# One order of attention's steps for another, with the first query load on ScalarE's queue

## The chip, the cores and the metric

The kernel runs on one core of one Trainium2 chip. The metric is the device time of one execution in microseconds (us). Five engines run side by side, each through its own list of instructions in order: TensorE (PE in the profile, with its weight loads as PEld), VectorE (DVE), ScalarE (ACT), GpSimd (POOL) and SyncE (SP), which here only issues DMAs. Engines wait for each other through semaphores alone.

## What is computed

Attention within clusters, then a mixture of experts over its output:

```python
q_assign = argmax(einsum('bhsd,hcd->bhsc', q / |q|, c / |c|))     # 16 clusters a head
k_assign = argmax(einsum('bhsd,hcd->bhsc', k / |k|, c / |c|))
scores = where(q_assign == k_assign, q @ k.T / sqrt(D), -1e9)     # B, H, S, D = 4, 8, 768, 64
x = softmax(scores) @ v                                           # as 3072 x 512
logits = x @ w_gate                                               # 8 experts
# tokens go to experts in order of falling logit, 384 to an expert; then, for each expert:
out[mask] = maximum(x[mask] @ w1[e], 0) @ w2[e]
```

## The kernel before

**Two lists of steps.** The program is written as two long strings of step names, one for attention and one for the experts. The first is named at L21. Each word of the string calls one small function, which issues a few instructions on one engine. So the string sets, by hand, in what order every engine meets its work; nothing else sorts it. Only the first string differs between the two kernels.

**Units.** Attention runs in 8 units u = 0 to 7, each of one batch and 4 heads. Per unit there are 24 tiles, each 128 keys or queries by all 768 of the other side.

- `load,u,k|q|v` fetches a unit by DMA (L488); unit 0's q and k come head by head, 192 KB each. `split_sc` (L630, ScalarE) multiplies a load by 64 in place, `split_hi` (L634, ScalarE) rounds it to half precision, and `split_lo` writes what the rounding lost. With the letter P, `split_lo` runs on GpSimd (L641) and wants the scaled load; with D, `split_hi` scales on its own and `split_lo` runs on VectorE (L639), so that no `split_sc` is needed. `dup` copies the rounded half into a second operand (`qb`, `kb`).
- `c0`, `c1`, `c2,0` to `c2,15`, `c3`, `c4` (L518 to L549) normalize the centroids: a chain of small VectorE operations with one square root on ScalarE (`c1`, L521), two transposes on TensorE (`c3`) and a copy into `ct` (`c4`).
- `cent0` and `cent` (L653) multiply queries and keys by the centroids on TensorE. `hh0` to `hh5` (unit 0) and `hot0` to `hot5` turn the products into cluster marks: four operations on VectorE (L675 to L681), one comparison there (L686) and one copy on ScalarE (L689, L691), which puts the marks beside the data in `qb`, `kb`.
- `pt` and `ptc` (L728, L732 or L734) transpose unit 0 on TensorE and copy the result out; later units are transposed by DMA (`trans`, L722).
- `m_mm` (L770) multiplies for one tile of queries the marked operands of all keys, and `m_rd` (L774, VectorE) takes the maximum of each row. There are 192 of each.
- `row0`, `row1` (L788, L792, VectorE) make three extra rows from the maxima of half a unit, `rowt` (L795) transposes them by DMA, and `row2` (L799) puts them by a second DMA into the query operand `qbt`, where `b_mm` reads them.
- `b_mm` (L809, L813) makes the scores of one tile, `b_exp` (L816, ScalarE) their exponentials, and `res` (L824) what their rounding to bf16 lost, on GpSimd (P) or VectorE (D). `av` (L846, L848, L827) multiplies by the values. `out0`, `out1`, `out2`, `hi0`, `hi1` (L856 to L879) divide and store.
- `m_mm`, `b_mm` and `pt` share three PSUM buffers named `sc`.
- `tab,n` is the n-th of a list of small constants, `offs` (L947) among them; `wgs` (L552, L553) splits the gate's weights. `misc` fills constants on GpSimd.
- `wd` (L660) is a product of 384 columns whose result nobody reads, before and between unit 0's steps.

In the steady part, the steps of unit u's `b_mm`, `b_exp`, `res` and `av` alternate with those of unit u+1's marks, `m_mm` and `m_rd`.

Of the kernel before, what the change touches and what calls it, by code (L numbers as in the profile page):

```python
# [26 lines left out]
split_hi,0,k,3,P split_lo,0,q,1,P wd c4 wd dup,0,q,1 cent0,0,k dup,0,k,1 cent0,0,q tab,14 split_lo,0,k,1,P wd dup,0,q,0
wd hh0,0 wd wd dup,0,k,0 hh1,0 wd split_lo,0,k,2,P wd split_hi,0,q,2,P hh2,0 pt,0,ka,1 pt,0,qa,1 hh3,0 split_sc,0,v,-
tab,12 wd split_lo,0,k,3,P ptc,0,ka,1,D pt,0,ka,2 wd ptc,0,qa,1,D wd wd wd hh4,0,q load,1,q,- wd hh4,0,k
split_hi,0,v,-,P tab,4 cent0,1,k wd wd wd cent0,1,q wd hh5,0,q tab,2 wd hh0,1 split_lo,0,v,-,P hh5,0,k wd split_sc,0,q,3  # L30
pt,0,qb,0 hh1,1 wd ptc,0,ka,2,A pt,0,kb,0 hh2,1 wd wd ptc,0,qb,0,A ptc,0,kb,0,D pt,0,ka,3 wd hh3,1 wd split_sc,1,k,-
m_mm,0,0 hh4,1,k hh4,1,q m_mm,0,1 m_rd,0,0 wd split_lo,0,q,2,P vs,0 load,2,k,- split_hi,0,q,3,P ptc,0,ka,3,D dup,0,k,3
split_lo,0,q,3,P m_rd,0,1 dup,0,k,2 pt,0,qa,2 vact,0 wd wd ptc,0,qa,2,D load,1,v,- vh2,0 m_mm,0,2 wd hh5,1,q vl2,0
pt,0,qa,3 split_hi,1,k,-,P m_rd,0,2 cent0,2,k cent0,2,q m_mm,0,3 hh0,2 wd hh5,1,k wd dup,0,q,2 split_lo,1,k,-,P
ptc,0,qa,3,D wd wd pt,0,qb,1 split_sc,1,q,- hh1,2 wd m_rd,0,3 pt,0,kb,1 wd wd wd hh2,2 wd ptc,0,kb,1,A m_mm,0,4 hh3,2 wd
wd hh4,2,k dup,0,q,3 wd ptc,0,qb,1,D wd wd split_hi,1,q,-,P m_rd,0,4 tab,31 m_mm,0,6 trans,1,ka,- zqm wd wd tab,10 wd
hh4,2,q m_mm,0,5 m_rd,0,6 hh5,2,q cent0,3,k hh5,2,k split_lo,1,q,-,P cent0,3,q m_mm,0,7 m_rd,0,5 wd wd wd wd hh0,3 wd wd
hh1,3 wd wd m_rd,0,7 pt,0,qb,2 m_mm,0,8 ptc,0,qb,2,A wd hh2,3 wd m_mm,0,9 trans,1,qa,- row0,0,0 hh3,3 split_sc,1,v,- wd
row1,0,0 hh4,3,k pt,0,qm,0 hh4,3,q m_rd,0,8 wd cent,1,k,0 ptc,0,qm,0,A cent,1,k,1 m_rd,0,9 cent,1,k,2 cent,1,k,3 hh5,3,q
split_hi,1,v,-,P pt,0,kb,2 hot0,1,k wd pt,0,qb,3 ptc,0,kb,2,D b_mm,0,0 hot1,1,k load,2,q,- hh5,3,k ptc,0,qb,3,A  # L40
pt,0,kb,3 load,2,v,- hot2,1,k wd wd ptc,0,kb,3,D b_exp,0,0 m_mm,0,11 hot3,1,k wd wd dup,1,q,- wd res,0,0,P m_rd,0,11
m_mm,0,10 wd wd m_mm,0,13 hot4,1,k m_mm,0,12 dup,1,k,- m_rd,0,10 split_lo,1,v,-,P cent,1,q,0 cent,1,q,1 wd m_rd,0,13 wd
wd split_hi,2,k,-,D m_mm,0,14 cent,1,q,2 m_rd,0,12 b_mm,0,2 cent,1,q,3 m_rd,0,14 b_exp,0,2 b_mm,0,1 hot0,1,q wd
m_mm,0,15 b_exp,0,1 row1,0,1 wd row0,0,1 hot1,1,q pt,0,qm,1 hot5,1,k tab,5 wd res,0,1,P m_rd,0,15 wd ptc,0,qm,1,A wd
trans,1,kb,- b_mm,0,3 hot2,1,q b_mm,0,5 b_exp,0,3 res,0,2,P hot3,1,q m_mm,0,16 b_exp,0,5 hot4,1,q wd wd m_mm,0,19
m_rd,0,16 hot5,1,q res,0,3,P b_mm,0,4 m_rd,0,19 b_mm,0,6 b_exp,0,4 trans,1,qb,- av,0,0 split_lo,2,k,-,D b_exp,0,6
m_mm,0,17 m_mm,0,18 vs,1 res,0,4,P m_rd,0,17 b_mm,0,7 m_rd,0,18 vact,1 m_mm,0,20 b_exp,0,7 row1,0,2 trans,2,ka,-
row0,0,2 m_mm,0,21 m_rd,0,20 av,0,1 split_hi,2,q,-,D res,0,7,P m_rd,0,21 m_mm,0,22 av,0,2 m_rd,0,22 vh2,1 pt,0,qm,2
res,0,5,P m_mm,0,23 ptc,0,qm,2,A av,0,3 m_rd,0,23 m_mm,1,0 b_mm,0,9 res,0,6,P load,3,k,- vl2,1 m_mm,1,1 m_rd,1,0
b_exp,0,9 av,0,4 av,0,5 m_rd,1,1 b_mm,0,8 row1,0,3 out0,0,0 tab,27 row0,0,3 m_mm,1,2 out1,0,0 b_exp,0,8 out2,0,0,D  # L50
b_mm,0,10 m_rd,1,2 hi0,0,0 cent,2,k,0 res,0,8,P b_mm,0,12 b_exp,0,10 hi1,0,0 m_mm,1,3 b_exp,0,12 m_mm,1,4 m_rd,1,3
res,0,9,P cent,2,k,1 split_hi,2,v,-,D cent,2,k,2 b_mm,0,11 m_rd,1,4 av,0,6 split_lo,2,q,-,D b_exp,0,11 m_mm,1,5 m_mm,1,6
dup,2,k,- cent,2,k,3 b_mm,0,14 m_rd,1,5 res,0,11,P av,0,7 trans,2,qa,- b_exp,0,14 av,0,8 hot0,2,k m_rd,1,6 b_mm,0,13
res,0,10,P av,0,9 hot1,2,k b_exp,0,13 pt,0,qm,3 hot2,2,k res,0,12,P m_mm,1,7 ptc,0,qm,3,A b_mm,0,15 hot3,2,k m_rd,1,7
load,3,q,- av,0,10 b_exp,0,15 res,0,13,P av,0,11 hot4,2,k b_mm,0,17 out0,0,1 out1,0,1 out2,0,1,D m_mm,1,8 res,0,14,P
b_exp,0,17 b_mm,0,16 m_rd,1,8 hi0,0,1 m_mm,1,9 b_exp,0,16 hi1,0,1 m_mm,1,10 res,0,15,P m_rd,1,9 hot5,2,k av,0,12 xtr,0,0
split_hi,3,k,-,D b_mm,0,18 m_rd,1,10 res,0,16,P m_mm,1,11 load,3,v,- av,0,13 m_rd,1,11 b_exp,0,18 m_mm,1,12 res,0,17,P
dup,2,q,- av,0,14 m_rd,1,12 b_mm,0,20 b_mm,0,19 res,0,18,D b_exp,0,20 av,0,15 row1,1,0 b_exp,0,19 row0,1,0
split_lo,2,v,-,D m_mm,1,13 rowt,1,0 lg0,0,0 av,0,16 av,0,17 res,0,19,P m_rd,1,13 b_mm,0,22 b_mm,0,21 out0,0,2 row2,1,0
out1,0,2 b_exp,0,22 tab,1 tab,22 m_mm,1,14 lg1,0,0 res,0,20,P trans,2,kb,- out2,0,2,D b_exp,0,21 cent,2,q,0 cent,2,q,1  # L60
m_rd,1,14 cent,2,q,2 hi0,0,2 cent,2,q,3 b_mm,1,0 res,0,22,P hot0,2,q hi1,0,2 m_mm,1,15 b_exp,1,0 b_mm,1,2 hot1,2,q
res,0,21,P m_rd,1,15 b_mm,0,23 av,0,18 hot2,2,q b_exp,0,23 split_lo,3,k,-,D av,0,19 b_exp,1,2 b_mm,1,1 m_mm,1,17
b_exp,1,1 res,0,23,P hot3,2,q m_mm,1,16 trans,3,ka,- av,0,20 m_rd,1,17 split_hi,3,q,-,D av,0,21 m_rd,1,16 res,1,0,P
m_mm,1,19 av,0,22 hot4,2,q av,0,23 m_rd,1,19 hot5,2,q b_mm,1,3 tab,8 res,1,2,P m_mm,1,18 out0,0,3 out1,0,3 b_exp,1,3
b_mm,1,4 trans,2,qb,- m_rd,1,18 res,1,1,P m_mm,1,20 b_exp,1,4 out2,0,3,D vs,2 hi0,0,3 res,1,3,P hi1,0,3 b_mm,1,5
m_rd,1,20 b_mm,1,6 b_exp,1,5 tab,24 xst,0,0 av,1,0 split_lo,3,q,-,D b_exp,1,6 m_mm,1,21 load,4,k,- av,1,1 vact,2
split_hi,3,v,-,D m_mm,1,22 b_mm,1,7 m_rd,1,21 res,1,6,P av,1,2 vh2,2 m_rd,1,22 m_mm,1,23 b_exp,1,7 res,1,4,P av,1,3
m_rd,1,23 m_mm,2,0 b_mm,1,9 row1,1,1 res,1,5,P m_rd,2,0 b_mm,1,8 b_exp,1,9 av,1,4 vl2,2 b_exp,1,8 m_mm,2,1 row0,1,1
res,1,7,P m_mm,2,2 rowt,1,1 m_rd,2,1 av,1,5 b_mm,1,10 out0,1,0 out1,1,0 res,1,8,P out2,1,0,D b_mm,1,11 b_exp,1,10
m_rd,2,2 cent,3,k,0 row2,1,1 hi0,1,0 cent,3,k,1 res,1,9,P b_exp,1,11 m_mm,2,4 hi1,1,0 xtr,0,1 cent,3,k,2 m_rd,2,4  # L70
dup,3,k,- m_mm,2,3 av,1,6 res,1,10,P m_rd,2,3 m_mm,2,6 trans,3,qa,- b_mm,1,12 m_rd,2,6 cent,3,k,3 res,1,11,P b_exp,1,12
m_mm,2,5 av,1,7 hot0,3,k hot1,3,k b_mm,1,14 res,1,12,P m_rd,2,5 av,1,8 b_exp,1,14 b_mm,1,13 hot2,3,k load,4,q,-
split_lo,3,v,-,D av,1,9 b_exp,1,13 xst,0,1 m_mm,2,7 b_mm,1,15 av,1,10 hot3,3,k res,1,13,P b_exp,1,15 m_rd,2,7 av,1,11
b_mm,1,16 out0,1,1 hot4,3,k res,1,15,P m_mm,2,8 out1,1,1 b_exp,1,16 b_mm,1,17 out2,1,1,D m_rd,2,8 lg0,0,1 hi0,1,1
res,1,16,P b_mm,1,18 b_exp,1,17 hi1,1,1 m_mm,2,9 b_exp,1,18 m_mm,2,11 xtr,1,0 av,1,12 tab,3 res,1,14,P m_rd,2,9
split_hi,4,k,-,D m_mm,2,10 av,1,13 lg1,0,1 m_rd,2,11 load,4,v,- res,1,17,P m_mm,2,12 dup,3,q,- av,1,14 m_rd,2,10 av,1,15
# [1395 lines left out]
```

## Time and profile before

| | us |
|---|---|
| median of 3 runs | 689.34 (689.24 to 691.9) |
| the profiled execution | 689.53 |
| its span, first to last instruction | 687.4 |
| mean granted TensorE clock | 0.976 of full speed |

| engine | busy us | share of the span |
|---|---|---|
| PE | 652.1 | 95% |
| DVE | 510.6 | 74% |
| POOL | 480.2 | 70% |
| ACT | 421.1 | 61% |

The time outside the span is 689.53 - 687.4 = 2.1 us. Attention takes the first 384 us or so, the experts the rest. A row of the timeline gives the start, the length, the engine, the line, what is written from what and how many instructions it stands for; the bracket at its end is the idle time of the engine ahead of it and who ended that. The ends of TensorE's products are modelled, so that a share of 95% does not say that it has no room: gaps shorter than a product's modelled tail are not seen.

### The profile page before, as it was taken

To read this page: it belongs to the slowest core of one execution; us is meant where nothing else is said; L and a number is where in the kernel's file an instruction comes from. 1 tells how busy PE (TensorE), PEld (TensorE's weight loads), DVE (VectorE), ACT (ScalarE), POOL (GpSimd) and SP (SyncE) were. 2 spreads that over 40 slices of the span, in tenths; PEclk is the share of its full clock that TensorE was granted. 3 is DMA by queue.
4 is the path that set the end of the run, shared out by engine and by line. 5 is a ranking of instruction groups with operands and counts; after the bars stand their busy time and mean duration, and the time that the engine had idled before them with its cause. 6 is when DMAs were issued, how large, how long until landed. Compare 5 with 4: busy or idle time off the path is not lost. (4 is left out here: it accounts for less than half of the span.)

```text
span 687.4 us, 19732 instructions
## 1 busy us (share of the span) xinstructions
PE 652.1 (95%) x8256; PEld 435.2 (63%) x8256; DVE 510.6 (74%) x1155; ACT 421.1 (61%) x554; POOL 480.2 (70%) x389
## 2 busy tenths in 40 slices
...
GB/s 197 175 176 149 173 198 135 166 156 182 165 164 142 133 178 203 98 104 89 74 27 71 25 144 150 269 70 315 128 292 140 244 204 179 245 331 175 46 1 46
DMA packets 175450, 105.84 MB, mean 154 GB/s; under 512 B 135426, under 2 KB 160002, under 8 KB 175362
## 3 DMA queue, kind: packets, MB, share of 16 engines
...
q14 instruction: 24, 0.20, 0.1%
...
## 5 line engine op out<-in xcount | busy, mean ns | idle before, releaser
L824 POOL TENSOR_TENSOR rt<-pt 128x768 f16<-128x768 f32 x174 | 260.8, 1524 | 77.8 <-ACT pt L816 72.2
L816 ACT ACTIVATE pt<-sc 128x768 f32<-128x768 f32 x192 | 150.6, 811 | 109.2 <-PE sc L813 106.2
L774 DVE TENSOR_REDUCE mxs<-sc 128x1 f32<-128x768 f32 x192 | 178.3, 949 | 17.0 <-PE sc L770 16.3
L1394 PE MATMUL pf<-xgt,w1h 128*128 128x384 f16 (+1 forms) x640 | 128.8, 293 | 0.3 <-DVE xgt L734 0.3
L846 PE MATMUL av<-vh,pt 128*128 128x66 f16 x1152 | 122.8, 194 | 0.1
L827 PE MATMUL av<-vh,rt 128*128 128x66 f16 x1152 | 122.5, 193 | 0.0
L848 PE MATMUL av<-vl,pt 128*128 128x64 f16 x1152 | 122.5, 192 | 0.0
L846 PEld LDWEIGHTS <-pt 128*128 128x128 bf16 x1152 | 106.4, 98 | 9.1 <-issue 0.2
L848 PEld LDWEIGHTS <-pt 128*128 128x128 bf16 x1152 | 105.8, 98 | 9.3 <-issue 0.9
L827 PEld LDWEIGHTS <-rt 128*128 128x128 f16 x1152 | 105.1, 97 | 0.0
L809 PE MATMUL sc<-qbt,kbt 99*128 99x384 f16 x384 | 93.8, 325 | 5.7 <-DMA qbt<-mt 4.1
L770 PE MATMUL sc<-kbt,qbt 80*128 80x384 f16 x384 | 91.0, 327 | 3.1 <-ACT pt L816 1.2
L813 PE MATMUL sc<-qat,kat 128*128 128x384 f16 x384 | 93.9, 325 | 0.0
L1394 PE MATMUL pf<-xgt,w1l 128*128 128x384 f16 (+1 forms) x320 | 89.9, 293 | 0.0
L1356 ACT ACTIVATE wr<-wr 128x1024 f32<-128x1024 f32 x64 | 66.7, 1046 | 25.2 <-DMA wr<-in_moe_w_dram 25.2
L1394 PEld LDWEIGHTS <-w1h 128*128 128x128 f16 x640 | 57.3, 97 | 28.7 <-issue 1.1
L1432 PE MATMUL pf<-w2h,hh 128*128 128x512 f16 x192 | 72.6, 378 | 0.0
L1432 PE MATMUL pf<-w2l,hh 128*128 128x512 f16 x192 | 72.5, 378 | 0.0
L1432 PE MATMUL pf<-w2h,hl 128*128 128x512 f16 x192 | 72.5, 378 | 0.0
L1366 POOL TENSOR_TENSOR w2l<-wr,w2h 128x1024 f16<-128x1024 f32 x32 | 67.6, 2132 | 1.7 <-ACT w2h L1359 1.2
L1366 POOL TENSOR_TENSOR w1l<-wr,w1h 128x1024 f16<-128x1024 f32 x32 | 67.5, 2137 | 0.2
...
## 6 DMA issues: line engine op xcount, KB each, us to landing
...
xg<-xrow,idx POOLq DMA_INDIRECT x24, 6.3
```

The lines of the kernel that those rows point to most:

```text
L770: nc.tensor.matmul(p[:, half, :S // 2], QBT[u][:D + C, i, :], KBT[u][:D + C, h * J + half * 3:h * J + half * 3 + 3, :], start=True, stop=True)
L774: nc.vector.tensor_reduce(mxs[u % 3][:, i:i + 1], MP.pop((u, i))[:, :, :S // 2], axis=AX.XY, op=OP.max)
L809: nc.tensor.matmul(ps[:, half, :S // 2], KBT[u][:ER + 3, s, :], QBT[u][:ER + 3, cs, :], start=True, stop=False)
L813: nc.tensor.matmul(ps[:, half, :S // 2], KAT[u][:, s, :], QAT[u][:, cs, :], start=False, stop=True)
L816: nc.scalar.activation(pts[(u * 12 + s // 2) % RP][:, s % 2], MP.pop((u, "b", s))[:, :, :S // 2], AF.Exp, scale=ESC)
L824: (nc.vector if e == "D" else nc.gpsimd).tensor_sub(rts[x][:, s % 2], p.rearrange("p a b -> p (a b)"), hi_view(pts[x])[:, s % 2])
L827: nc.tensor.matmul(o[:, j, :], r[:, j * P:(j + 1) * P], VH[u][:, s, :], start=False, stop=(s % J == J - 1), skip_group_check=True)
L846: nc.tensor.matmul(o[:, j, :], hi[:, js], VH[u][:, s, :], start=(kt == 0 and j == 0), stop=False, skip_group_check=True)
L848: nc.tensor.matmul(o[:, j, :D], hi[:, js], VL[u][:, s, :], start=False, stop=False, skip_group_check=True)
L1366: nc.gpsimd.tensor_sub(lo, wrs[c], hi)
L1394: nc.tensor.matmul(o, (w1l if i == 2 else w1h)[x][:, c, fs], xgt[x][:, h + int(i == 1), ts], start=(first and i == 0), stop=(last and i == ...
L1432: nc.tensor.matmul(PS["o", p, g], (hl if i == 2 else hh)[x][:, f, g * P:(g + 1) * P], (w2l if i == 1 else w2h)[x][:, f, :], start=(f == 0 ...
```

## The change

The string of steps for attention is replaced by another order of nearly the same steps; the experts' string is the same. The code changes in four places: `load` can issue on ScalarE's queue, the fill of `onesh` becomes a step of its own (`ones`) which is called third of GpSimd's fills, `wd` multiplies `onesh` by itself instead of by the table `wt`, and the first heads of q and k (`split_hi,0,q,0`, `split_hi,0,k,0` and their `split_lo`) go from P to D, so that two `split_sc` fall away. The number of `wd` is the same. Of the 192 `res`, 18 ran on VectorE and 16 do now; in units 0 to 6 it is 8 before and 6 after, in unit 7 it is 10 in both.

```diff
-zqb loadc misc load,0,k,0 loadg load,0,q,0 load,0,k,2 c0 c1 load,0,k,1 c2,0 c2,1 load,0,q,1 c2,2 c2,3 load,0,k,3 c2,4
...
+ident load,0,q,0,A split_hi,0,q,0,D ones load,0,k,0 wtio wd loadc wd tab,0 misc wd tab,4 load,0,k,3 wd load,0,k,2 wd
...
-    def load(u, name, hh):
+    def load(u, name, hh, e=None):
...
-        nc.sync.dma_start(LD[name, u][:, hs, :], ap)
+        (nc.scalar if e == "A" else nc.sync).dma_start(LD[name, u][:, hs, :], ap)
...
+    def ones():
+        nc.gpsimd.memset(onesh, 1.0)
+
     def fills():
-        nc.gpsimd.memset(onesh, 1.0)
...
-        nc.tensor.matmul(PC["d"], onesh, wt.rearrange("p t c -> p (t c)"), start=True, stop=True)
+        nc.tensor.matmul(PC["d"].rearrange("p (a b) -> p a b", b=P), onesh, onesh[:, None, :].to_broadcast([P, T * C // P, P]), start=True, stop=True)
```

Three places where the order of an engine's instructions differs:

ScalarE, from the program's start. The row with `ss` is the centroids' square root (`c1`); `ld_76` holds q and `ld_75` k of unit 0, and `qa`, `ka` are their split forms. A minus stands before, a plus after.

```order
+L488 DMA ld_76<-in_q_dram 128x384
+L636 ACT_TABLE_LOAD
+L636 ACTIVATE qa<-ld_76 128x6x64 [waits DMAHW0_49]
 L521 ACT_TABLE_LOAD
 L521 ACTIVATE ss<-ss 128x1 [waits DVE_49]
-L630 ACTIVATE ld_76<-ld_76 128x384 [waits DMAHW3_49]
-L634 ACTIVATE qa<-ld_76 128x6x64 [waits Activation_49]
-L630 ACTIVATE ld_75<-ld_75 128x384 [waits DMAHW1_49]
-L630 ACTIVATE ld_75<-ld_75 128x384 [waits DMAHW4_49]
```

The load of q and its rounding stand ahead of the square root now, and there is a second table load between the rounding and the root.

VectorE, from the program's start (the rows with `ss`, `sq` and `cst` are the centroids' chain).

```order
+L949 TENSOR_SCALAR offs_158<-ji 128x32 [waits Pool_49]
+L641 SCALAR_TENSOR_TENSOR qa<-ld_76,qa 128x6x64 [waits DMAHW0_49,Activation_49]
+L518 SCALAR_TENSOR_TENSOR sq,ss<-cf 128x64 [waits DMAHW2_49]
 L526 TENSOR_SCALAR ss<-ss 128x1 [waits Activation_49]
 L526 RECIPROCAL ss<-ss 128x1 [waits DVE_49]
 L526 TENSOR_TENSOR ss<-ss 128x1 [waits DVE_49] x2
+L641 SCALAR_TENSOR_TENSOR ka<-ld_75,ka 128x6x64 [waits DMAHW1_49,Activation_49]
 L526 TENSOR_SCALAR ss<-ss 128x1 [waits DVE_49]
-L552 TENSOR_SCALAR wg<-wgf 128x4x8 [waits DMAHW2_49]
-L553 SCALAR_TENSOR_TENSOR wg<-wgf,wg 128x4x8 [waits DVE_49]
-L526 RECIPROCAL ss<-ss 128x1
```

One `offs` table and the two `split_lo` of the first heads have come in ahead of and into the chain; the split of the gate's weights has left it (it comes in unit 2 now), and the copy of `qat`, which stood inside the chain, follows it.

VectorE, where the extra rows of unit 2's second half are made (`m_94`), before:

```order
204 L792 TENSOR_SCALAR m_94<-mxs_142 128x12x2 [waits DMAHW2_49,DVE_49]
205 L788 TENSOR_SCALAR m_94<-mxs_142 128x12x2
206 L639 SCALAR_TENSOR_TENSOR vl_110<-ld_77,vh_107 128x1536 [waits DMAHW1_49,Activation_49]
207 L774 TENSOR_REDUCE mxs_140<-sc 128x1 [waits PE_49]
208 L761 SCALAR_TENSOR_TENSOR vm_124<-vmh,rest,mx 2x4x64 [waits Activation_49]
209 L947 TENSOR_SCALAR tri<-ji 128x128 [waits Pool_49]
210 L856 TENSOR_SCALAR rc<-av 128x6 [waits PE_49]
211 L859 RECIPROCAL rc<-rc 128x6 [waits DVE_49]
212 L867 TENSOR_TENSOR av<-av,rc 128x6x64 [waits DVE_49]
```

and after, from the last of the two rows:

```order
203 L790 TENSOR_SCALAR m_94<-mxs_142 128x12x2
204 L641 SCALAR_TENSOR_TENSOR vl_110<-ld_77,vh_107 128x1536 [waits DMAHW0_49]
205 L776 TENSOR_REDUCE mxs_140<-sc 128x1 [waits PE_49]
206 L858 TENSOR_SCALAR rc<-av 128x6 [waits PE_49]
207 L861 RECIPROCAL rc<-rc 128x6 [waits DVE_49]
208 L869 TENSOR_TENSOR av<-av,rc 128x6x64 [waits DVE_49]
209 L776 TENSOR_REDUCE mxs_140<-sc 128x1 [waits PE_49]
210 L881 TENSOR_TENSOR xb_146<-av,xb_146 128x6x64 [waits DMAHW7_49,DMAHW4_49,Activation_49]
211 L776 TENSOR_REDUCE mxs_140<-sc 128x1 [waits PE_49] x2
```

The first `b_mm` that reads these rows (`b_mm,2,12`) is called right behind row 212 before, and behind the first of the two reductions of row 211 after. The string of before has two `m_mm`, three `b_mm`, two `av` and two `cent` between the rows and this reader, that of after four, one, three and four.

## Rows read from the trace of the kernel before

**Rows 1.** Busy time by stretches: length, then PE, PEld, DVE, ACT, POOL, clock, DMA.

```profile
20.00:344.00 324.00, 314.36 (x5225) 234.42 (x5224) 299.58 (x490) 215.13 (x283) 253.26 (x183) 0.99 0.72 150
344.00:384.00 40.00, 36.75 (x719) 28.68 (x715) 29.45 (x54) 20.46 (x30) 21.10 (x17) 1.00 0.19 42
```

**Rows 2.** Waits of DVE from 20 to 344 us: total us, times, longest.

```profile
DVE mxs L774 <- PE sc L770: 15.9, 32, 1.1
```

**Rows 3.** Timeline of DVE at the start: start, length, what, idle before.

```profile
3.17 0.15 DVE L526 TENSOR_SCALAR ss<-ss 128x1 f32<-128x1 f32 x1 [0.27 <-ACT ss L521]
...
4.22 0.19 DVE L553 SCALAR_TENSOR_TENSOR wg<-wgf,wg 128x32 f16<-128x32 f32 x1
...
9.89 0.56 DVE L734 COPY qat<-sc 128x768 f16<-128x768 f16 x1 [4.45 <-PE sc L728]
...
12.49 0.27 DVE L549 COPY ct<-mx 128x256 f16<-128x256 f16 x1
13.60 0.36 DVE L675 TENSOR_REDUCE cmx<-mx 128x12 f32<-128x192 f32 x1 [0.83 <-PE mx L653]
...
16.39 3.09 DVE L947 TENSOR_SCALAR offs<-ji 128x32 f32<-128x32 int32 x2
...
21.71 0.95 DVE L774 TENSOR_REDUCE mxs<-sc 128x1 f32<-128x768 f32 x1
```

**Rows 4.** Timeline of ACT, at the start and at the first exponential.

```profile
0.76 1.28 ACT L521 ACT_TABLE_LOAD   x1 [0.76 <-PEq L1458]
2.93 0.20 ACT L521 ACTIVATE ss<-ss 128x1 f32<-128x1 f32 x1 [0.89 <-DVE sq L518]
5.59 0.52 ACT L630 ACTIVATE ld<-ld 128x384 f32<-128x384 f32 x1 [2.45 <-DMA ld<-in_q_dram]
...
18.66 0.81 ACT L732 ACTIVATE qbt<-sc 128x768 f16<-128x768 f16 x1 [0.75 <-PE sc L728]
...
39.13 1.28 ACT L816 ACT_TABLE_LOAD   x1
40.42 0.81 ACT L816 ACTIVATE pt<-sc 128x768 f32<-128x768 f32 x1
```

**Rows 5.** Timeline of SP's first issues, and of PE's and DVE's first rows.

```profile
0.76 0.41 SPq L508 DMA_DIRECT2D cf<-in_centroids_dram  x1
...
2.17 0.51 SPq L488 DMA_DIRECT2D ld<-in_q_dram  x1
...
2.67 0.23 DVE L518 SCALAR_TENSOR_TENSOR sq<-cf 128x64 f32<-128x64 f32 x1 [2.67 <-DMA cf<-in_centroids_dram]
...
6.14 3.36 PE L660 MATMUL av<-wt,onesh 128*128 128x384 f16 x10 [6.14 <-POOL wt L556]
...
12.22 0.65 PE L660 MATMUL av<-wt,onesh 128*128 128x384 f16 x3
```

**Rows 6.** Groups of instructions to 384 us: form, count, busy us, mean ns.

```profile
L824 DVE TENSOR_TENSOR rt<-pt 128x768 f16<-128x768 f32 x18 | 19.0, 1084 | 0.5
...
L639 DVE SCALAR_TENSOR_TENSOR ka<-ld,ka 128x1536 f16<-128x1536 f32 x6 | 10.6, 1758 | 0.0
```

**Rows 7.** Waits of PE from 62 to 384 us.

```profile
PE sc L809 <- DMA qbt<-mt: 4.1, 4, 1.5
```

**Rows 8.** Timeline at unit 2's and unit 7's second half: extra rows made, first reader.

```profile
146.33 0.22 DVE L788 TENSOR_SCALAR m<-mxs 128x24 f16<-128x24 f32 x1
...
152.28 0.50 PE L809 MATMUL sc<-qbt,kbt 99*128 99x384 f16 x2 [1.35 <-DMA qbt<-mt]
...
356.12 0.22 DVE L788 TENSOR_SCALAR m<-mxs 128x24 f16<-128x24 f32 x1
...
362.09 0.50 PE L809 MATMUL sc<-qbt,kbt 99*128 99x384 f16 x2 [1.47 <-DMA qbt<-mt]
```

**Rows 9.** Busy time by stretches around unit 2's wait (columns as in the first group).

```profile
152.00:154.00 2.00, 1.72 (x14) 1.02 (x15) 1.35 (x4) 1.06 (x2) 2.00 (x3) 0.69 0.90 172
154.00:156.00 2.00, 2.00 (x42) 1.66 (x40) 1.68 (x2) 1.61 (x2) 2.00 (x2) 0.50 1.14 211
```

More of the change, by code (lines that the diff above doesn't have):

```diff
@@ L27 @@
[L27 to L76, printed above, removed]
@@ L182 @@
[L182 to L184 removed]
+ident load,0,q,0,A split_hi,0,q,0,D ones load,0,k,0 wtio wd loadc wd tab,0 misc wd tab,4 load,0,k,3 wd load,0,k,2 wd
+load,0,k,1 wd load,0,q,1 split_lo,0,q,0,D load,0,q,2 pt,0,qa,0 c0 load,0,v,- c1 split_hi,0,k,0,D c2,0 load,1,k,- wd c2,1
@@ new lines @@
+m_mm,0,5 dup,0,q,3 vl2,0 wd wd hh5,1,k wd m_rd,0,3 dup,0,q,2 cent0,2,k cent0,2,q pt,0,kb,1 hh0,2 wd m_rd,0,5 wd
+ptc,0,kb,1,A trans,1,ka,- wd wd pt,0,qa,3 split_sc,1,q,- wd hh1,2 m_mm,0,7 ptc,0,qa,3,D wd wd hh2,2 wd wd wd hh3,2 wd
+split_hi,1,q,-,P m_mm,0,4 hh4,2,k hh4,2,q m_rd,0,7 cent0,3,k cent0,3,q wd hh5,2,q wd hh0,3 split_lo,1,q,-,P hh5,2,k wd
+load,2,k,- m_rd,0,4 pt,0,qb,2 m_mm,0,6 ptc,0,qb,2,A wd wd hh1,3 wd m_rd,0,6 wd split_sc,1,v,- wd pt,0,kb,2 wd m_mm,0,9
+hh2,3 wd hh3,3 wd wd ptc,0,kb,2,D wd wd trans,1,qa,- m_mm,0,8 hh4,3,q hh4,3,k hh5,3,q wd m_rd,0,9 split_hi,1,v,-,P
@@ new lines @@
+cent,1,k,0 cent,1,k,1 cent,1,k,2 m_rd,0,8 cent,1,k,3 wd hh5,3,k pt,0,qb,3 hot0,1,k m_mm,0,11 ptc,0,qb,3,A row1,0,0
+row0,0,0 hot1,1,k pt,0,qm,0 m_rd,0,11 wd wd ptc,0,qm,0,A wd load,2,q,- wd wd pt,0,kb,3 hot2,1,k load,2,v,- dup,1,q,-
+b_mm,0,0 ptc,0,kb,3,D m_mm,0,10 hot3,1,k wd wd m_rd,0,10 b_exp,0,0 wd wd wd m_mm,0,13 hot4,1,k res,0,0,P wd wd m_mm,0,12
+m_rd,0,13 hot5,1,k cent,1,q,0 dup,1,k,- wd m_mm,0,14 m_rd,0,12 split_lo,1,v,-,P cent,1,q,1 cent,1,q,2 cent,1,q,3
+m_rd,0,14 split_hi,2,k,-,D m_mm,0,15 trans,1,kb,- b_mm,0,2 m_rd,0,15 b_mm,0,1 b_exp,0,2 hot0,1,q m_mm,0,16 wd row0,0,1
@@ new lines @@
+b_exp,0,1 row1,0,1 wd hot1,1,q res,0,2,P wd pt,0,qm,1 m_rd,0,16 b_mm,0,3 ptc,0,qm,1,A hot2,1,q b_mm,0,5 res,0,1,P
+b_exp,0,3 hot3,1,q wd m_mm,0,17 b_exp,0,5 hot4,1,q b_mm,0,4 split_lo,2,k,-,D hot5,1,q vs,1 split_hi,2,q,-,D trans,1,qb,-
+wd m_rd,0,17 res,0,5,P m_mm,0,19 b_exp,0,4 wd m_rd,0,19 m_mm,0,18 b_mm,0,6 res,0,4,P m_rd,0,18 m_mm,0,20 b_exp,0,6
+av,0,0 trans,2,ka,- m_mm,0,21 row1,0,2 row0,0,2 m_rd,0,20 b_mm,0,7 av,0,1 m_rd,0,21 b_exp,0,7 m_mm,0,22 split_hi,2,v,-,D
+av,0,2 res,0,7,P m_rd,0,22 pt,0,qm,2 m_mm,0,23 b_mm,0,8 ptc,0,qm,2,A m_rd,0,23 tab,35 load,3,k,- res,0,3,P vact,1
@@ new lines @@
+b_mm,0,9 load,3,q,- vh2,1 b_exp,0,8 vl2,1 m_mm,1,0 av,0,3 m_rd,1,0 b_exp,0,9 res,0,8,P av,0,4 m_mm,1,1 av,0,5 m_rd,1,1
+res,0,6,P b_mm,0,10 out0,0,0 m_mm,1,2 out1,0,0 b_exp,0,10 out2,0,0,D b_mm,0,11 res,0,9,P m_rd,1,2 hi0,0,0 cent,2,k,0
+m_mm,1,4 b_exp,0,11 cent,2,k,1 cent,2,k,2 dup,2,k,- row1,0,3 tab,12 row0,0,3 hi1,0,0 res,0,10,P b_mm,0,13 m_rd,1,4
+m_mm,1,3 av,0,6 b_exp,0,13 m_rd,1,3 res,0,11,P cent,2,k,3 b_mm,0,12 hot0,2,k b_mm,0,14 b_exp,0,12 split_lo,2,q,-,D
+av,0,7 b_exp,0,14 m_mm,1,6 av,0,8 res,0,12,P hot1,2,k m_mm,1,5 load,3,v,- m_rd,1,6 m_mm,1,7 trans,2,qa,- av,0,9 hot2,2,k
@@ new lines @@
+out0,0,3 m_rd,1,19 trans,2,qb,- vs,2 b_exp,1,3 res,1,1,P out1,0,3 m_rd,1,18 m_mm,1,20 out2,0,3,D b_mm,1,5 res,1,3,P
+m_rd,1,20 hi0,0,3 b_mm,1,4 b_exp,1,5 hi1,0,3 b_mm,1,6 b_exp,1,4 split_lo,3,q,-,D m_mm,1,23 av,1,0 b_exp,1,6 m_mm,1,21
+b_mm,1,7 m_rd,1,23 res,1,5,P av,1,1 b_exp,1,7 m_rd,1,21 m_mm,1,22 res,1,4,P vact,2 av,1,2 split_hi,3,v,-,D m_rd,1,22
+b_mm,1,8 av,1,3 row1,1,1 row0,1,1 res,1,6,D b_exp,1,8 rowt,1,1 m_mm,2,0 b_mm,1,9 vh2,2 m_rd,2,0 res,1,8,P m_mm,2,1
+load,4,q,- b_exp,1,9 av,1,4 m_rd,2,1 av,1,5 res,1,7,P row2,1,1 vl2,2 b_mm,1,10 out0,1,0 m_mm,2,2 xtr,0,1 out1,1,0
@@ new lines @@
+out2,1,0,D b_exp,1,10 b_mm,1,11 tab,14 m_rd,2,2 tab,22 hi0,1,0 res,1,9,P cent,3,k,0 cent,3,k,1 b_exp,1,11 m_mm,2,4
+hi1,1,0 cent,3,k,2 dup,3,k,- m_rd,2,4 m_mm,2,3 res,1,10,P m_mm,2,6 trans,3,qa,- av,1,6 m_rd,2,3 cent,3,k,3 b_mm,1,13
+res,1,11,P hot0,3,k m_rd,2,6 av,1,7 b_exp,1,13 b_mm,1,12 tab,11 split_lo,3,v,-,D b_mm,1,14 b_exp,1,12 m_mm,2,5
+b_exp,1,14 av,1,8 xst,0,0 res,1,13,P hot1,3,k m_mm,2,7 split_hi,4,k,-,D m_rd,2,5 av,1,9 xst,0,1 av,1,10 load,4,v,-
+m_rd,2,7 res,1,14,P b_mm,1,15 hot2,3,k av,1,11 b_exp,1,15 b_mm,1,16 hot3,3,k res,1,12,P out0,1,1 m_mm,2,8 out1,1,1
```

245 lines of the change are left out of this document (132 added, 113 removed).

## The prediction

> **What bounds the kernel now.** I read the busy time by stretches first [rows 1]. From 20 to 344 us, the steady part of attention, VectorE works 299.58 of 324 us, 92%; GpSimd 78%, ScalarE 66%. TensorE's row says 97%, but its ends are modelled, so I asked the waits which engine is late. VectorE waits 15.9 us in all for the products whose row maxima it takes, in 32 waits, the longest 1.1 us [rows 2]. So VectorE is the nearest bound, and its waits for TensorE fill most of what is left. From 344 us on (unit 7's end) VectorE has 29.45 of 40 us and TensorE is the bound; little changes there.
>
> The start is a chain. VectorE's second half of the centroids' normalization stands behind a copy that waits 4.45 us for TensorE [rows 3]; TensorE waits for unit 0's first split, that for q, which lands at 5.59 us [rows 4]. The marks (first reduction at 13.60) and the first row maximum (21.71) follow [rows 3].
>
> One kind of stall recurs: TensorE's `b_mm` waits four times, 4.1 us in all, for the extra rows' DMA into `qbt` [rows 7]. From the end of the rows' making to the first reader it is 152.28 - 146.33 - 0.22 = 5.73 us in unit 2 and 362.09 - 356.12 - 0.22 = 5.75 us in unit 7 [rows 8]. So two DMAs one behind the other take 5.7 us, and a stall comes wherever less work is put between.
>
> **The change part by part.** All terms go against the profiled execution, 689.53 us, which stands 0.2 above the median of 689.34; outside its span lie 2.1 us, which I leave as they are.
>
> *The start.* q is issued on ScalarE's queue at 0.76 at the earliest, where its table load stood. How long it then takes the trace shows for two loads: 1.91 us for the centroids (0.76 to 2.67) and 3.42 us for q itself (2.17 to 5.59) [rows 4, 5]. q would land between 2.67 and 4.18; I take 3.9, near its own row. Its rounding takes one pass of 0.52 [rows 4], to 4.42; then the second table load, 1.28 [rows 4], to 5.70; the square root and its hand-over 0.24 (2.93 to 3.17), to 5.94. The chain on VectorE thus begins 2.8 us later than before. It took 2.27 us, from 3.17 to the start of the idle time at 9.89 - 4.45 = 5.44 [rows 3]. It loses the gate's split, two operations of 0.19 or less [rows 3], some 0.3, and takes in k's `split_lo`, a quarter of a row of 1758 ns [rows 6], 0.44: it ends at 8.35. By then q's transposition no longer waits for GpSimd, since q's `split_lo` is on VectorE. From the copy of `qat` to `ct` it was 12.49 - 9.89 = 2.60 us, to the first reduction 1.11 more [rows 3]: 12.06 against 13.60, so **-1.5**. Bounds: -2.7 with q at 2.67. On the other side q at 4.18 costs 0.3, and the order has six dummy products ahead of `cent0` in place of three; the ten at the start took 0.336 each, the three 0.65 together [rows 5], so six could cost 6 x 0.336 - 0.65 = 1.4 more, and the gain is nil.
>
> A rule speaks against this part: the Trainium skill, "ScalarE: Activation LUTs", section "What ACT_TABLE_LOAD costs", gives about 1283 ns for a load and a drain of some 1380 ns for every switch to another set. Here the exponential's load begins at 39.13, lasts 1.28, and the first exponential starts at 40.42 [rows 4], so no drain is seen; by the page the sum would end 1.3 us higher.
>
> *Tables and gate split.* Two `offs` tables took 3.09 us at 16.39, in the middle of the marks [rows 3]. One, now VectorE's first instruction, falls into time in which it waits for q. Half of 3.09 leaves the dense stretch; another small table comes in there, so **-1.0** (bounds -1.5 and -0.5). The gate's split goes into a full stretch: **+0.3**.
>
> *`res`.* Two leave VectorE, at 1.08 each [rows 6]: **-2.2**; GpSimd with its 78% takes them. The other bound is nil: if a score's `res` then comes later, `av` waits as long.
>
> VectorE's sum is -1.5 - 1.0 + 0.3 - 2.2 = -4.4 us. It is the bound for 92% of the stretch [rows 1]: **-4.1** on the end. The cover that must stay is TensorE's own work, discussed last.
>
> *The extra rows.* I counted, for each of the 14 half units with extra rows, the rows of VectorE ordered between the making and the first reader, with the durations of the trace. Before, nine of 14 lie below 5.75 us; after, two (5.2 in unit 6, 4.5 in unit 7), the rest at 6.1 or more. Unit 2's second half shows it: behind the same `split_lo` (1.76 [rows 6]) the changed order has three row maxima of 0.95 ahead of the reader or beside it, the old one had one. Of the 4.1 us of waits [rows 7], that of unit 2 (1.35) and two of unit 7 would go or shrink: I take -1.1, -0.3 and -0.6, **-2.0**. Around unit 2's wait the granted clock fell to 0.69 and 0.50 of full speed, that is down to the 1.2 GHz level, after TensorE had stood waiting [rows 9]; VectorE lost about 1 us there too, so the gain may be up to -5. It is nil where VectorE's lag hid the wait from the end anyway.
>
> *New waits.* A new order of some 2,000 steps moves every wait. No row of before shows these. VectorE faster by 4.4 us meets TensorE's products a little earlier and will wait more often; I give back a quarter of the 4.4 and some for displaced stalls: **+1.5**. Bounds: -2, if the better spread of `m_mm` (runs of four or more fall from ten to three) spares some of the 15.9 us of [rows 2], and +5, a third of these 15.9 again.
>
> Removing two `split_sc` from ScalarE and two `split_lo` from GpSimd, and the dummies' other operand, I cost at nothing beyond the start: both engines have a fifth to a third of the stretch free [rows 1]. Dummies no longer wait for GpSimd's table until 6.14 [rows 5], which can only bring TensorE's clock up earlier.
>
> Sum: -4.1 - 2.0 + 1.5 = -4.6; 689.53 - 4.6 = **684.9 us**.
>
> **The rivals.**
>
> *All favourable bounds hold.* q lands at 2.67 (-1.2 more), and the waits fall by 2 us rather than rise: about 681.5. Against it: a load of q's size has its own row, at 3.42 us.
>
> *The lead is lost on its way (the change does not do at the start what it says).* The first row maximum needs `qbt`'s copy on ScalarE as well, which came at 18.66, behind a long queue of splits [rows 4]. If that queue, or q's load behind other issues, still sets 21.71, the start's -1.5 and -1.0 are gone, and so is some of what `res` frees, since unit 0 then waits for loads. Only the extra rows' -2.0 stay: 687.5. For it: ScalarE is busy without a gap to 18.66 but for 0.75 us.
>
> *A table load holds ScalarE for twice its row.* The square root waits 1.3 us longer, and VectorE's chain with it; x 0.92 = +1.2: 686.1. The row at 40.42 speaks against it [rows 4]. This is the page's drain as a mechanism of this kernel.
>
> *Slower: VectorE starves on `m_mm`.* The order alternates `m_mm` and `m_rd` closely, with fewer products made ahead. A wait of VectorE lasted 15.9 / 32 = 0.5 us [rows 2]. With the forecast's allowance of 1.5 taken out, the order gains 6.1 us; from 12 further waits of that size on it is no gain, and with 19 (9.5 us) it is slower by 3.4 us: about 693. Against it: VectorE's 92% leave only 24 us of idle time in 324 [rows 1], so 9.5 more would be much; for it: in a list of fixed order one late product holds all behind it, exponentials too.
>
> **How the numbers follow.** About 0.5%, 3.4 us, is what a measurement of this kernel can tell from no change: faster is below 685.9, slower above 692.8. The forecast has 0.52, its own range being 682.5 to 687.5, with 0.44 of it below 685.9. The favourable bounds have 0.06, the lost lead 0.24, the doubled table load 0.06, starving 0.12. Faster: 0.44 + 0.06 = 0.50. Same: 0.08 + 0.24 + 0.06 = 0.38. Slower: 0.12. The range reaches from 681.0, below the favourable case, to 689.0, above the lost lead and its spread; it leaves out starving and the rim of the others, some 0.17.
>
> **What would show it.** Right: q's landing before 4.2, a table load of 1.28 ahead of the square root and no idle time behind it, VectorE's first marks near 12 and first row maximum near 19.5; `res` on VectorE 16 times; TensorE's waits for `qbt` near 2 us instead of 4.1, no fall of the clock near unit 2; VectorE's waits for `sc` below 20 us. Wrong: a first row maximum at 21 or later (lost lead), a gap behind the second table load, or VectorE's waits for `sc` at 25 us or more (starving). If the start's lead is seen at 22 us but not at 344, the order has given it back in between, and the table of stretches shows where.

## The result: 680.0 us, more than twice the forecast gain

| | before | changed |
|---|---|---|
| median | 690.62 us (4 runs, 689.24 to 692.91) | 679.96 us (4 runs, 678.96 to 681.54) |
| ratio | | 0.9844, 95% interval 0.9807 to 0.9882 |
| profiled execution | 689.53 | 678.96 |
| its span | 687.4 | 677.2 |

The direction was right. The size was not: I forecast 684.9 with 681.0 as the lower end, and the kernel lies below that end. Between the two profiled spans lie 10.2 us. I place them by landmarks that both kernels have, such as the last row maximum (`m_rd`) of a unit and the last `av`; a lag is the changed kernel's time less the old one's, both read from the traces.

| landmark | before, us | lag, us |
|---|---|---|
| first row maximum | 21.7 | -3.7 |
| last one of unit 0 | 57.6 | -2.3 |
| last one of unit 2 | 144.5 | -4.7 |
| last one of unit 5 | 273.4 | -5.5 |
| last one of unit 7 | 355.1 | -8.3 |
| last `av` | 380.2 | -9.0 |
| end of the span | 687.4 | -10.2 |

So 2.3 us come from the start, 6.7 from the steady part and unit 7, and 1.2 from the experts, whose steps were not touched.

### The profile page after: what moved, and what is told of

Its sections match the earlier page's. It is cut to its first block, busy times and chain, and to the rows that moved or that the text cites. A ratio compares the mean times of both kernels' runs of the same rounds, so it can differ in the third digit from the quotient of the medians.

```text
span 677.2 us, 19698 instructions
## 1 busy us (share of the span) xinstructions
PE 651.2 (96%) x8256; PEld 434.8 (64%) x8256; DVE 506.4 (75%) x1155; ACT 421.9 (62%) x553; POOL 485.1 (72%) x389
## 5 line engine op out<-in xcount | busy, mean ns | idle before, releaser
L826 POOL TENSOR_TENSOR rt<-pt 128x768 f16<-128x768 f32 x176 | 267.5, 1546 | 63.9 <-ACT pt L818 63.6
L776 DVE TENSOR_REDUCE mxs<-sc 128x1 f32<-128x768 f32 x192 | 178.8, 951 | 13.5 <-PE sc L772 11.9
```

Source lines behind the costliest of these rows:

```text
L776: nc.vector.tensor_reduce(mxs[u % 3][:, i:i + 1], MP.pop((u, i))[:, :, :S // 2], axis=AX.XY, op=OP.max)
L826: (nc.vector if e == "D" else nc.gpsimd).tensor_sub(rts[x][:, s % 2], p.rearrange("p a b -> p (a b)"), hi_view(pts[x])[:, s % 2])
```

## The profile after

The start, on ScalarE and then VectorE, in the timeline of the changed kernel (start, length, what, idle before), beside [rows 3, 4]:

```profile
0.76 0.39 ACTq L488 DMA_DIRECT2D ld<-in_q_dram  x1
1.19 1.28 ACT L636 ACT_TABLE_LOAD   x1 [1.19 <-PEq L1460]
3.85 0.52 ACT L636 ACTIVATE qa<-ld 128x384 f16<-128x384 f32 x1 [1.38 <-DMA ld<-in_q_dram]
4.39 1.28 ACT L521 ACT_TABLE_LOAD   x1
5.68 0.20 ACT L521 ACTIVATE ss<-ss 128x1 f32<-128x1 f32 x1
```

```profile
2.23 0.52 DVE L949 TENSOR_SCALAR offs<-ji 128x32 f32<-128x32 int32 x1 [2.23 <-POOL ji L952]
...
5.92 0.15 DVE L526 TENSOR_SCALAR ss<-ss 128x1 f32<-128x1 f32 x1 [0.81 <-ACT ss L521]
...
8.68 0.30 DVE L526 CAST cst<-sq 128x64 f16<-128x64 f32 x2
...
10.12 0.28 DVE L549 COPY ct<-mx 128x256 f16<-128x256 f16 x1
11.24 0.36 DVE L677 TENSOR_REDUCE cmx<-mx 128x12 f32<-128x192 f32 x1 [0.83 <-PE mx L655]
...
18.06 2.73 DVE L776 TENSOR_REDUCE mxs<-sc 128x1 f32<-128x768 f32 x3
```

q landed at 3.85, the root began right behind the second table load at 5.68, and the chain at 5.92. The forecast had 3.9, 5.70 and 5.94. Up to here each step came as worked out. Then `ct` came at 10.12 and not 10.95, mainly since the two casts took 0.30 us; in the old kernel they took 1.17, beside a `split_lo` of GpSimd, which had nothing to do at that time in the changed one. The last section tells why that matters.

The waits of TensorE behind unit 0, to the last `av` of the old kernel (57 to 381 us: total us, times, longest). In the old kernel these two stand beside the wait of [rows 7]:

```profile
PE mx L653 <- DMA kat<-ka: 1.4, 2, 0.9
...
PE mx L907 <- DMA xt<-xb: 0.5, 1, 0.5
```

and these are the longest in the changed one. Its last `av` comes at 371 us, so that the first two lie behind attention:

```profile
PE sc L897 <- ACT xb L877: 1.7, 1, 1.7
PE pc L1166 <- DVE oh L1014: 1.4, 1, 1.4
PE mx L655 <- DVE L L924: 1.4, 2, 1.0
PE sc L772 <- DVE mxs L776: 0.4, 1, 0.4
```

All three kinds of wait for a DMA, 4.1 + 1.4 + 0.5 = 6.0 us, are gone, and nothing of that size has come in their place. VectorE's waits for `sc` fell too, in the stretch of [rows 2]:

```profile
DVE mxs L776 <- PE sc L772: 11.9, 22, 1.9
```

Last, busy times from unit 0's end to the last `av` (length, then PE, PEld, DVE, ACT, POOL, clock, DMA), before and then changed:

```profile
57.55:380.22 322.67, 314.45 (x5469) 237.38 (x5466) 290.20 (x469) 203.66 (x269) 252.99 (x185) 0.99 0.65 135
```

```profile
55.29:371.19 315.90, 313.35 (x5480) 237.67 (x5479) 287.50 (x472) 203.46 (x270) 260.17 (x191) 0.99 0.67 138
```

The length falls by 6.8 us. TensorE's busy time falls by 1.1 and its idle time by 5.7, from 322.67 - 314.45 = 8.2 to 315.90 - 313.35 = 2.5. VectorE's busy time falls by 2.7 and its idle time by 4.1. In each of the two traces the granted clock fell once in this stretch, so that the clock does not make the difference. That speaks for TensorE as the bound and against my reading of [rows 1], but two columns that both fall decide nothing. The experiments had to.

## The experiments

Two theories stand against each other. V: VectorE sets the pace, as the prediction says. T: TensorE does, and each microsecond in which it stands idle is one of the end; I came to it only in the course of the runs, and the one that gives TensorE more work is its test. Since executions of the old kernel differ by several microseconds (below), I read the median for the verdict and the landmarks for the place.

**The start alone.**

```diff
-zqb loadc misc load,0,k,0 loadg load,0,q,0
...
-m_rd,0,0
+ident load,0,q,0,A split_hi,0,q,0,D ones load,0,k,0
...
+m_rd,0,1
```

> The changed order up to its first row maximum (the first 147 steps), then the rest in the order of before. Theory V (VectorE binds from the first row maximum to unit 7, so a lead at the start is carried to the end): first row maximum near 18.1 us instead of 21.7, end 3.0 to 4.0 us earlier than before, some 686.0 against 689.5. Rival L (the lead is lost in unit 0, where the marks and loads set the pace): first row maximum early, end within 1 us of before. Rival F (my forecast's size): 2.3 us earlier.

Measured: 683.99 us against 690.83, ratio 0.9891 (0.9857 to 0.9926). The first row maximum came at 18.0. The lag was -2.2 us at the end of unit 0, and it stayed there through 300 us of the same order: -2.3 at 144 us, -2.4 at 230, -3.0 at 316, -2.7 at the last `av`, -3.7 at the end. So a lead, once past unit 0, is carried to the end of attention nearly one to one, and the rival that it is lost falls. Of the 3.7 us at the first row maximum 1.5 were gone by the end of unit 0; that this is only an earlier place in unit 0's order, with other work of unit 0 behind it, is my reading and not shown. The median moved by more than this trace, 6.8 us; the section on the hardware comes back to that.

**The order alone.**

```diff
+zqb loadc misc load,0,k,0 loadg load,0,q,0
...
+m_rd,0,0
-ident load,0,q,0,A split_hi,0,q,0,D ones load,0,k,0
...
-m_rd,0,1
```

> The order of before up to its first row maximum (the first 150 steps, with its loads, dummy products and first heads), then the rest in the changed order. Theory V: what is left of the change's 10.2 us when the start's 3.7 are away: about 6.5 earlier than before, some 683.0, of which 1.2 only if the clock's return at 400 us comes early again. Forecast's sizes: -2.2 x 0.92 for the two res, -2.0 for the extra rows, +1.5: 2.5 earlier, some 687.0.

Measured: 683.06 us, ratio 0.9877 (0.9842 to 0.9912), 7.8 us faster. At the joint it lost time (first row maximum 23.5, unit 0's end at 60.3). From there to the last `av`:

```profile
60.32:376.43 316.11, 312.02 (x5480) 237.12 (x5479) 286.31 (x469) 203.47 (x270) 259.95 (x189) 1.00 0.66 137
```

That is 316.1 us, as in the changed kernel and 6.6 less than before, with 4.1 us of TensorE idle. But here the clock stayed full in this stretch, where it fell once in both of the others, at a price of some 1.2 us (last section). So the order is worth 5 to 7 us, not the 2.5 of my terms.

**The readers of the extra rows, moved in the old kernel.**

```diff
-b_mm,2,0 hi0,1,2 res,1,22,P hi1,1,2 m_mm,2,15 b_exp,2,0
+hi0,1,2 res,1,22,P hi1,1,2 m_mm,2,15 b_mm,2,0 b_exp,2,0
...
-b_mm,2,12 m_rd,3,2 hi0,2,0 m_mm,3,4 res,2,8,P b_exp,2,12 cent,4,k,2 hi1,2,0 cent,4,k,3 m_mm,3,3 m_rd,3,4
+m_rd,3,2 hi0,2,0 m_mm,3,4 res,2,8,P cent,4,k,2 hi1,2,0 cent,4,k,3 m_mm,3,3 b_mm,2,12 b_exp,2,12 m_rd,3,4
...
-b_mm,7,0 b_exp,6,23 hi1,6,2 m_mm,7,15 b_exp,7,0 av,6,18
+b_exp,6,23 hi1,6,2 m_mm,7,15 av,6,18 b_mm,7,0 b_exp,7,0
...
-b_mm,7,14 hi0,7,0 b_mm,7,12 res,7,10,P b_exp,7,11 hi1,7,0 av,7,6 b_exp,7,12 av,7,7
+av,7,6 av,7,7 b_mm,7,14 hi0,7,0 b_mm,7,12 res,7,10,P b_exp,7,11 hi1,7,0 b_exp,7,12
```

> The kernel before with only the four places mended where TensorE waits for the extra rows (units 2 and 7): the first readers stand some products later. Theory W (my forecast: these waits are half on the path): 2.0 us earlier, at most 4.1. Theory V: TensorE's waits for qbt fall from 4.1 us to under 1, the end moves by 0 to 1.5 us, and only by the two in unit 7, where TensorE binds; VectorE's idle time from the first to the last row maximum stays near 24.8 us.

Measured: 689.77 us, ratio 0.9978 (0.9947 to 1.0009): no clear change. In the trace unit 2's second half gained 1.8 us (lag from +1.2 to -0.6); about 1.1 of it fell where the old kernel's clock was at half and this one's was not. Over the whole stretch the waits changed their name or their place (TensorE, 62 to 385 us):

```profile
PE sc L809 <- DMA qbt<-mt: 2.6, 3, 1.4
PE sc L809 <- DVE mxs L774: 2.6, 3, 1.0
PE av L846 <- DVE xb L879: 2.0, 3, 1.2
```

At the edited places the waits for the rows' DMA were down to 0.2 us in all, but waits of 0.7, 0.5 and 1.2 us for VectorE stood near three of them, and two new ones for the DMA came in units 5 and 6, which I had not edited. TensorE's idle time rose from 8.2 to 9.9 us, so the run tests neither theory. It shows that moving the readers alone did not mend these waits here.

**Half the order**: the changed order up to unit 4's first `m_mm`, and from there what is left of the old one.

```diff
-zqb loadc misc load,0,k,0 loadg load,0,q,0
...
+ident load,0,q,0,A split_hi,0,q,0,D ones load,0,k,0
...
 m_mm,4,0
...
```

> The changed order up to unit 4's first m_mm, then the order of before. By the two traces the changed kernel is 4.7 us ahead at 189.5 us. Theory V (a lead is kept): 4 to 5.5 us earlier than before at the end, some 684.8. Rival (leads are levelled out by the next wait): under 2 us earlier.

Measured: 689.19 us, ratio 0.9981 (0.9949 to 1.0014). The lag was -5.9 us at 189.5 and -1.4 at 208.5, and then between -1.1 and -1.8 for 170 us. The loss lies at the joint, where TensorE stood still for 0.99 us for an exponential at 187.5 and the clock fell behind it:

```profile
192.00:194.00 2.00, 1.85 (x52) 1.55 (x51) 1.97 (x4) 1.19 (x2) 1.77 (x3) 1.00 1.09 206
194.00:196.00 2.00, 2.00 (x25) 1.29 (x23) 2.00 (x3) 0.00 (x0) 1.55 (x2) 0.60 1.10 225
196.00:198.00 2.00, 2.00 (x22) 1.32 (x21) 1.97 (x4) 0.81 (x1) 0.19 (x1) 0.55 0.96 235
```

The rival had the better number (1.6 us earlier by the medians), but not for its reason: the lead was lost at the cut and not levelled out wait by wait. So the run does not tell what the first half is worth; it shows again that a lag, once there, stays.

**Fewer and more `res` on VectorE**, in the changed kernel.

```diff
-res,1,6,D
+res,1,6,P
...
-res,6,22,D
+res,6,22,P
```

> The changed kernel with the six res of units 0 to 6 that run on VectorE given to GpSimd. Theory V (VectorE binds): 6 x 1.04 = 6.2 us less work, the end 4 to 6 us earlier than the changed kernel, some 675. Rival P (GpSimd, 84% busy between, becomes the bound, and av waits for res): no gain, or up to 6 us slower, some 680 to 686.

```diff
-res,2,18,P
+res,2,18,D
...
-res,5,10,P
+res,5,10,D
```

> The changed kernel with four res more on VectorE (units 2 to 5, one each), so 20 in place of 16. Theory V: 4 x 1.04 = 4.2 us more work, the end 4 us later than the changed kernel, some 684. Rival P (the balance with GpSimd is flat here): within 1 us.

Measured: 681.13 us with six fewer and 680.90 with four more, 8.7 and 9.0 us below the old kernel in the same set (689.86), where the changed kernel was 10.7 below in its own set. Both edits cost a little rather than one of them gaining. Busy times from the first row maximum to the last `av`, of the changed kernel, with six fewer, and with four more:

```profile
18.06:371.19 353.13, 348.42 (x5908) 261.75 (x5906) 321.92 (x530) 235.10 (x310) 282.00 (x201) 1.00 0.69 144
```

```profile
17.92:372.36 354.44, 347.27 (x5908) 261.26 (x5907) 317.87 (x524) 235.20 (x310) 290.06 (x207) 1.00 0.69 144
```

```profile
17.92:371.72 353.80, 348.03 (x5908) 261.53 (x5906) 325.01 (x534) 235.11 (x310) 277.18 (x197) 1.00 0.69 144
```

VectorE's busy time goes from 321.9 to 317.9 or to 325.0, and the length from 353.1 to 354.4 or 353.8. Theory V wanted 6 us less and 4 more. The clock fell once in the changed kernel's stretch and not in these two; beside the run with the root first (below), whose clock stayed full as well and whose stretch took 351.7 us, they are 2.7 and 2.1 us longer. With six fewer, what VectorE saved it waited, and V falls here. Four more cost about half of their 4.2 us: behind unit 0 TensorE stood idle for 3.6 us in place of 2.5. So VectorE's work is not free either, where TensorE waits for it.

With six fewer, two waits of TensorE for the extra rows had come back, at 107 and 354 us:

```profile
PE sc L811 <- DMA qbt<-mt: 2.6, 2, 1.4
```

This gives the price of such a wait, though the run was not made for it. From unit 0's end to the last `av`, first with the root first and then with six fewer:

```profile
55.00:369.47 314.47, 311.93 (x5481) 237.29 (x5480) 287.39 (x472) 203.38 (x270) 260.05 (x191) 1.00 0.67 138
```

```profile
55.15:372.36 317.21, 312.20 (x5480) 237.18 (x5479) 283.45 (x466) 203.56 (x270) 268.23 (x197) 1.00 0.67 137
```

These two and the order alone have the same products, a full clock and nearly the same other waits of TensorE there (2.1 to 2.3 us). For the extra rows' DMA it waited 0, 2.6 and, in the order alone, 1.7 us; the stretch took 314.5, 317.2 and 316.1 us. Each of these waits is carried one to one to the last `av`.

**More work on TensorE**, in the changed kernel.

```diff
-        for half in range(2):
+        for half in ((0, 0, 1) if u in (3, 4) else (0, 1)):
             nc.tensor.matmul(p[:, half, :S // 2], QBT[u][:D + C, i, :],
```

> The changed kernel in which each m_mm of units 3 and 4 writes its first half twice: 48 more products of 384 columns on TensorE, 0.16 us each, nothing more for another engine. Theory T (TensorE sets the pace from the first row maximum to the last av; VectorE's idle time is what is left over): 48 x 0.16 = 7.8 us later than the changed kernel, some 687.5. Theory V (VectorE binds, TensorE has room): 0 to 2 us later.

Measured: 684.54 us, 5.6 us or more above the three kernels that ran beside it, which have the changed order without these products (678.71 to 678.94). From unit 0's end:

```profile
55.12:375.98 320.86, 319.23 (x5528) 241.54 (x5527) 286.35 (x472) 203.54 (x270) 259.96 (x191) 1.00 0.67 135
```

Against the kernel with filled gaps below, whose clock did not fall in this stretch either (314.87 long, 312.08 busy), it is 6.0 us longer: 7.1 us more of work, 0.15 for each product, less 1.1 us of waits that this work covers. VectorE did no more, and waited 7 us more (34.5 in place of 27.5). GpSimd did no more either (259.96 and 260.01 us), which rules out rival P, GpSimd as the bound, for this kernel. So theory T holds in the changed kernel: work for TensorE alone made the stretch longer by most of it.

**One small operation earlier**, in the changed kernel.

```diff
+lg2,1,1
 split_lo,5,k,-,D
...
-lg2,1,1
```

> The changed kernel with one small VectorE operation (lg2 of unit 1, 0.19 us, on which TensorE's cent waits 0.99 us at 166.2 and, behind it, 0.42 for an m_mm) moved ahead of the split_lo of 1.74 us. Theory T: TensorE's wait goes, 1.0 to 1.4 us earlier, and up to 1.3 more where the clock no longer falls behind it (as at 168.3 in the trace), some 678. Theory V: VectorE does the same work, 0.

Measured: 678.94 us, no different from the runs beside it. TensorE's 0.99 and 0.42 us at 166 to 167 became (155 to 175 us)

```profile
PE sc L772 <- DVE mxs L776: 1.6, 1, 1.6
```

The idle time is the same, only its name is another. Both names stand behind one VectorE operation, which took 1.50 us in place of 0.22 in both traces (last section). The expected gain of 1.0 to 1.4 us is refuted; to remove the named wait was not to remove its cause.

**Tables, table load and gaps.** Three more, each one edit: the two `offs` tables early in the old kernel; a first square root that loads the root's table while q is on its way; and dummy products in the gaps behind the last `av`.

```diff
+tab,4 tab,2
 ptc,0,qa,0,D
```

> The kernel before with one edit: the two offs tables, which took 3.0 us at 16.4 us, stand ahead of the first copy of qat, where VectorE is idle. Theory H (such an operation of VectorE stands still until GpSimd's running operation ends, and the 3.0 us end with GpSimd's split_lo of v at 19.37): each takes 0.2 to 0.6 us in the new place, the first row maximum comes 2 to 3 us earlier, and the end as much (a lead is carried one to one, as in start_only), some 687.5 against 690. Theory F (my forecast: a price of 1.5 us each and a gain of half a row): the two take 3 us in the idle time too, and the end gains 1 us.

```diff
+        nc.scalar.activation(wq, onesh[:, 0:1], AF.Sqrt)
```

> The changed kernel with a square root of one column put ahead of the first rounding on ScalarE, so that the root's table is loaded while q is on its way and no second load stands ahead of the centroids' root. VectorE's first sum of squares was there at 5.10 and the root began at 5.68: the chain begins up to 0.5 us earlier. Lead carried one to one: 0.5 earlier at the end than the changed kernel. Rival: another input of the marks is late then, 0.

```diff
+wx,9
 out0,7,3 out1,7,3 out2,7,3,D
...
+wx,5
 lg0,7,1 lg1,7,1 lg2,7,1
...
+wx,9
```

> The changed kernel with 23 dummy products of 384 columns (0.16 us each) in the places behind the last av where TensorE waits 1.7 and 1.5 us (371 to 378 us). Theory C (the clock falls at 376.5 because TensorE stands still there, and the experts' start is paid at half clock): it falls later or not at all, and the stretch from the last av to the end shrinks from 306.0 by 1 to 3 us. Rival: it falls all the same in the thin stretch behind, 0, or up to 1 us later by the products that stand in the way.

Measured, tables: 690.66 us against 689.86, ratio 1.0006 (0.9984 to 1.0028). In the trace the two took 0.56 us together where they had taken 3.09 [rows 3], the first row maximum came 1.5 us earlier, less than the 2 to 3 of theory H, and the lag stayed, -1.7 at 355 us. The executions scatter by 6.6 us, and the median does not show it.

```profile
5.58 0.56 DVE L947 TENSOR_SCALAR offs<-ji 128x32 f32<-128x32 int32 x2 [0.17 <-POOL ji L950]
```

Root first: the root began at 5.19, 0.49 earlier, but `cent0` then waited 1.15 us in place of 0.83, and the first mark came 0.18 earlier. 679.30 us; the run cannot tell that from the changed kernel.

Filled gaps: 678.91 us, not told apart from the changed kernel either. The clock fell about 5 us later (381 in place of 376.5), but the stretch from the last `av` to the end took 307.0 us and not less than 306.0. Theory C falls: what counts there is when the clock comes back (last section).

**All three together.**

> The changed kernel with the square root's table first, the early lg2 and the filled gaps together. If the three gains add up (0.5, 1.0 to 2.6 and 1 to 3 us): 674 to 677.5 against 680. If the fill costs instead: 678 to 680.

Measured: 678.71 us (678.35 to 681.58), ratio to before 0.9855 (0.9826 to 0.9883). The gains do not add up, and no version here is clearly faster than the changed kernel.

## Why the prediction was wrong

1. *What bounds the kernel* is the step that failed. [rows 1] gave TensorE 97% and VectorE 92%. I set TensorE's row aside since its ends are modelled, and took VectorE's waits for `sc` [rows 2] as what is left over. They were the evidence against me: VectorE waited 15.9 us for TensorE, and TensorE waited 1.4 us for row maxima behind unit 0. The engine that was waited for longer set the pace. The run with more products shows it (6.0 us longer for 7.1 us of work), and six fewer `res` show that it was not VectorE. Both are runs of the changed kernel; that TensorE binds the old one too was not tested by itself and is inferred from its idle time, which makes 5.7 of the 6.8 us. That idle time, 8.2 us behind unit 0, was the measure of what an order could gain.

2. *The start*, -1.5 - 1.0 + 0.3, times 0.92, made -2.0; at the end of unit 0 it is -2.3, and -2.2 with the start alone. The sum came out, but partly by luck: the first mark came 2.4 us earlier (13.60 to 11.24) and not 1.5, since the casts were no longer held up, and of what the tables were to add nothing was left at the end of unit 0. The factor of 0.92 had no ground, since the lead was carried nearly one to one. The landing of q and the second table load came within 0.05 us. The rival of a doubled table load falls, since the root starts 0.01 us after the load's end, and so does that of the lost lead.

3. *`res`*, -2.2: no gain to be seen (with six fewer the stretch was 2.7 us longer, not 6 shorter, and TensorE's waits for the extra rows account for it). A saving on an engine that waits for another is waited away.

4. *The extra rows*, -2.0: I halved the four waits because VectorE's lag might hide them, and left out the waits for `kat` and `xt`, which the same answer of the trace held. All 6.0 us of DMA waits went, and TensorE's idle time fell by 5.7. This is the term that was mis-sized most. The mechanism, more work between the rows' making and their reader, is as the prediction counted it; in the changed order a wait for the extra rows cost its full length (order alone, six fewer), so that halving it was wrong. That the old kernel's waits were all on the path in the same way is inferred, since the run that moved its readers made other waits.

5. *New waits*, +1.5: none. TensorE's idle time is less than what the gone waits leave, and VectorE's waits for `sc` fell by 4 us in 20 to 344 us, against a forecast that gave 1.5 back.

6. *The experts*, nothing in the sum: -1.2, by the clock's return.

7. *The range*. The favourable case is added up wrongly. With q at 2.67 (-1.1 after the factor) and the waits at -2 in place of +1.5 it is 684.9 - 1.1 - 3.5 = 680.3 us and not 681.5; with the bounds that I gave for the tables (-1.5) and the extra rows (-5) as well, 676.9. The lower end of 681.0 rests on that slip, and the result lies below it.

With TensorE as the bound the sum would have been the measured -2.3 for the start and -4 to -6 for the waits, some 682, inside the range that I gave. What stays open is about 1 us between unit 0 and the last `av`, by which TensorE's modelled busy time fell at a nearly equal count of products. "Starving on `m_mm`" was far off: VectorE's waits for these products fell from 15.9 to 11.9 us.
